# Global rows by TENSOR_REDUCE, global values scaled on ScalarE, w_in behind v's fifth transfer, and a newly planned order, in local and global attention with a softplus MLP

## The chip, the cores and the metric

The kernel runs on one core of one Trainium2 chip. The metric is device time in microseconds, the median of several runs. Beside it stands one profiled execution with its trace; all numbers of the trace below come from that one.

The engines, as the profile names them: PE (TensorE: matmuls; PEld are its weight loads), DVE (VectorE), ACT (ScalarE), POOL (GpSimd) and SP (SyncE, here only a queue for DMA). Each runs its own instructions in order and waits on semaphores for the others.

## The reference

Attention over 8 batches of 8 heads, 576 positions, head size 64. Each position sees a window of 32 on both sides and 8 global positions; the global positions see everything and are seen by everything. An MLP with a softplus follows.

```python
def _attn_ref(q, k, v, global_idx) -> np.ndarray:
    window = 32
    scores = scale * np.matmul(q, k.transpose(0, 1, 3, 2))
    mask = np.abs(pos[:, None] - pos[None, :]) <= window
    mask = mask | is_global[:, None] | is_global[None, :]
    scores = np.where(mask, scores, -1000000000.0)
    scores = scores - np.max(scores, axis=-1, keepdims=True)
    attn = np.exp(scores)
    attn = attn / (np.sum(attn, axis=-1, keepdims=True) + 1e-09)
    return np.matmul(attn, v).astype(np.float32)

def _moe_ref(x, w_in, w_out) -> np.ndarray:
    h = x @ w_in
    g = np.maximum(h, 0.0) + np.log1p(np.exp(-np.abs(h)))
    return (g @ w_out).astype(np.float32)
```

`x` is the attention's output as 4608 tokens of 512 channels; `w_in` is 512 by 2048, `w_out` 2048 by 512.

## The kernel before

**Tiling.** A block is 32 positions of one batch with all 8 heads; four blocks make a pair `n` (128 rows, 36 pairs), four pairs make a tile `m` of 512 tokens (9 tiles). For a pair PE computes scores `s` (L960), DVE adds the mask into `st` (L964) and takes the row maximum `m` (L977; for the first four pairs from `s`, L975), POOL subtracts it (L983), ACT takes the exponential (L996, L992), DVE the sum `sm` and its reciprocal `rs` (L1003, L1005), POOL multiplies into `pn` (L1011), DVE transposes into `pt` (L1020). PE then forms the values `xo` (L1122) of a piece of a tile, `xT` is copied out (L622, the line of a helper), and the MLP follows: `h` (L1157, weights `win`), softplus `g` on ACT (L1163), `o` (L1168, weights `wout`), a copy `osb` and a store.

**The global path**, once per batch `b`, gives the attention of the 8 global positions. PE computes their scores `sg` (L860) in four pieces; DVE takes four maxima `gm` (L870) and joins them by two into `gnb` (L871); ACT takes exponentials into `pg` (L877); DVE transposes `pg` into `pgt` (L882) and copies the one-hot rows `own`, which tell where a global position lies, beside it (L884); PE multiplies with v, `ov` (L893), which also sums the weights and gathers v; the odd blocks' half is copied to `odd` (ACT or DVE), DVE adds the even half (L904), takes the reciprocal `grs` (L905) and scales into `vg` (L906). PE's `xo` needs `vg`, and v in bf16, `vb`, which POOL, DVE or ACT casts from the landed `stage2`.

ACT holds one table at a time: exponential or softplus; a switch is an ACT_TABLE_LOAD.

**Loads.** SP issues q, k and v of a batch; v in eight transfers, four of them for each half of the heads (L370). The weights go through POOL's queue: `w_in` in four pieces behind a small copy `seen` (L1236) that waits until v's second transfer of batch 0 has landed, `w_out` in four pieces behind a like copy for the last q of batch 1. Batch 1's loads on SP stand behind a tiny read of `w_in`'s second piece (`trail`, L653), v of batch 1 behind one of `w_out`'s second.

**The order.** Nothing is emitted as it is written. Every piece of work is a job with costs in ns (begin to next, begin to end) for each engine that may do it, with dependencies, a rank and the buffers and PSUM banks that it opens. `_Order.run` takes the job that can start first by its own clock, the rank breaking ties, and so fixes the engine of each job and the order of each engine. `DRAWS` disturbs ranks and gives some jobs a `hold`, their earliest start after what they wait for. `stall` models that PE reads its own instructions in blocks of 256, which are asked for at instruction 130 and needed at 442, then every 256 further, and take the times in `SLOW`. Idle stretches of PE up to 34 us are filled with matmuls on nothing (`warm`, L630).

Of the kernel before, what the change touches and what calls it, by code (L numbers as in the profile page):

```python
# [282 lines left out]
def kernel(  # L283
# [49 lines left out]
    DRAWS = (14983,88331,14823,89303,53658,33409,90561,3122,88327,96354,15096,44709,93792,39917,99844,80902,91136,6210,80107,65898,80098,28397,56976,32762,97173,31915,3965,53549,42749,35567,44889,97522,97233,49667,59144,12623,98256,77249,34126,)  # L333
# [347 lines left out]
    def add_cast(b, w):  # L681
# [6 lines left out]
        for h in range(2):  # L688
# [158 lines left out]
    def add_global(b, gate):  # L847
# [15 lines left out]
        def mx(e, hs):  # L863
# [7 lines left out]
            V.tensor_tensor(out=PS["gnb", b][:, hs[0]:hs[-1] + 1], in0=m[:, hs[0]:hs[-1] + 1, 0], in1=m[:, hs[0]:hs[-1] + 1, 1], op=OP.min)  # L871
# [9 lines left out]
        def tpg(e, m0, m1):  # L881
            V.transpose(out=pgt[:, m0:m1].rearrange("p m i h -> p (m i h)").bitcast(I32),  # L882
                        in_=pg[:, m0:m1].rearrange("p m i h -> p (m i h)").bitcast(I32))
            V.tensor_copy(pgt[:, m0:m1, NG:2 * NG, :].rearrange("p m g h -> p m (g h)"),  # L884
                          own[:, m0:m1].rearrange("p m g h -> p m (g h)"))
# [15 lines left out]
        def gv(e):  # L901
            rs = sb.tile([P, 1], FP32, tag="grs", name="grs")
            both = PS["odd", b]
            V.tensor_tensor(out=both[:], in0=PS["ov", b, 0][:, :], in1=both[:], op=OP.add)  # L904
# [1 line left out]
            V.tensor_scalar(out=vg[i][:], in0=both[:, 0:2 * D], scalar1=rs[:, 0:1], scalar2=None, op0=OP.mult)  # L906
# [434 lines left out]
```

## Time and profile before

| what | us |
|---|---|
| median of three runs | 355.19 |
| the three runs | 352.88, 355.19, 356.19 |
| the profiled execution | 355.85 |
| its span, from first to last instruction | 354.1 |
| mean granted TensorE clock | 0.971 of full speed |

In the page, busy time is a share of the span, and a group's line gives the count, the busy time, the mean of one in ns, the idle time of the engine just before, and what ended that idle time. In a timeline a row gives start, duration, engine, line, operation, output and input, the count, and in brackets the idle time before with its releaser. In the waits, a row gives who waited for whom, the total, the number of times and the longest.

### The profile page before, as it was taken

Reading aid. Unit: us, or ns where it says so; the run is one execution under the profiler, and the core shown is the slowest. Engines: PE = TensorE matmul, PEld = TensorE weight load, DVE = VectorE, ACT = ScalarE, POOL = GpSimd, SP = SyncE. Lnnn points to the kernel's source line nnn. Section 1 sums busy time; section 2 is a strip of 40 time slices with the busy share of each in tenths; the row PEclk is TensorE's granted clock in tenths of the full one; section 3 lists DMA queues with packets and bytes.
Section 4 is the critical chain, followed back from the end, with each engine's and each line's share of the span. In section 5 each row is a group of like instructions: output and inputs, shape, how many; then the busy total and the mean of one; then the engine's idle time right before and its main releaser. Section 6 shows DMA issues by size and latency. Waiting matters only on the chain.

```text
span 354.1 us, 12267 instructions
## 1 busy us (share of the span) xinstructions
PE 323.5 (91%) x5327; PEld 171.8 (49%) x5327; DVE 238.9 (67%) x397; ACT 235.8 (67%) x463; POOL 188.5 (53%) x167
## 2 busy tenths in 40 slices
PE   6828769989997999899979998999999989999996
PEld 3414748458744444444435444544454454445453
DVE  7767668893899799994898089967991691061000
ACT  5658746969793779358926693679576837754631
POOL 6555627656296685569459535875954342060000
PEclk9667989999999999999999999999999999999999
DMA  7999799994999988925977098610100010010011
GB/s 194 198 204 255 142 213 165 173 187 108 180 181 199 193 157 140 189 66 120 183 131 181 15 178 153 164 35 31 61 33 31 22 70 32 0 59 33 30 44 74
DMA packets 168733, 42.74 MB, mean 121 GB/s; under 512 B 153192, under 2 KB 165736, under 8 KB 168680
## 3 DMA queue, kind: packets, MB, share of 16 engines
q1 hardware_dynamic: 160664, 28.33, 45.3%
q0 software_dynamic: 6144, 10.49, 12.3%
q10 hardware_dynamic: 1872, 3.15, 2.4%
q8 instruction: 41, 0.67, 0.8%
q14 instruction: 12, 0.10, 0.1%
HBM read 36.71 MB, written 9.44 MB: 130 GB/s over the span
## 4 chain that ended last, share of the span: by engine, by line
PE 51%; DVE 25%; SPq 10%; ACT 6%; DMA 4%; issue 3%; DVEq 0%; ACTq 0%
PE h L1157 30%; PE o L1168 13%; DVE sm L1003 7%; SPq L365 5%; DVE pt L1020 4%; PE xo L1122 4%; DMA stage<-in_v_dram 4%; SPq L370 3%; DVE pgt L884 3%; DVE vg L906 3%; PE s L960 2%; ACT st L996 2%; DVE gm L870 1%; DVE pgt L882 1%; ACT g L1163 1%
## 5 line engine op out<-in xcount | busy, mean ns | idle before, releaser
L1168 PE MATMUL o<-wout,g 128*128 128x512 bf16 (+1 forms) x592 | 134.0, 374 | 0.0
L1157 PE MATMUL h<-xT,win 128*128 128x512 bf16 (+2 forms) x768 | 133.8, 328 | 0.0
L1011 POOL TENSOR_TENSOR pn<-st,rs 128x1024 bf16<-128x1024 f32 (+1 forms) x39 | 68.1, 1754 | 81.5 <-DVE rs L1005 69.4
L1163 ACT ACTIVATE g<-h 128x512 bf16<-128x512 f32 (+2 forms) x192 | 86.0, 499 | 33.5 <-PE h L1157 30.3
L1157 PEld LDWEIGHTS <-win 128*128 128x128 bf16 x768 | 69.1, 98 | 56.4 <-issue 1.1
L1168 PEld LDWEIGHTS <-g 128*128 128x128 bf16 x592 | 55.2, 98 | 61.2 <-issue 1.4
L983 POOL TENSOR_TENSOR st<-st,m 128x1024 f32<-128x1024 f32 x32 | 60.3, 1894 | 29.4 <-DVE m L977 29.4
L1003 DVE TENSOR_REDUCE sm<-st 128x8 f32<-128x1024 f32 x32 | 38.0, 1188 | 18.3 <-ACT st L996 18.1
L964 DVE TENSOR_TENSOR st<-s,mask 128x512 f32<-128x512 f32 x64 | 40.7, 675 | 5.1 <-PE s L960 5.0
L622 ACT COPY osb<-o 128x512 f32<-128x512 f32 (+1 forms) x37 | 21.1, 572 | 28.3 <-PE o L1168 22.8
L977 DVE TENSOR_REDUCE m<-st 128x8 f32<-128x1024 f32 x32 | 38.3, 1207 | 0.2
L996 ACT ACTIVATE st<-st 128x1024 f32<-128x1024 f32 x32 | 32.5, 1057 | 1.4 <-POOL pn L1011 0.9
L622 ACT CAST xT<-xo 128x512 bf16<-128x512 f32 (+2 forms) x25 | 11.8, 528 | 22.2 <-PE xo L1122 22.1
L1020 DVE STREAM_TRANSPOSE pt<-pn 128x512 int32<-128x512 int32 x36 | 24.6, 688 | 1.7 <-POOL pn L1011 1.6
L870 DVE TENSOR_REDUCE gm<-sg 128x1 f32<-128x320 f32 (+1 forms) x32 | 12.4, 448 | 12.8 <-PE sg L860 12.7
L1180 POOL DMA_DIRECT2D out_dram<-osb x24 | 14.1, 589 | 11.0 <-ACT osb L622 5.9
L717 DVE STREAM_TRANSPOSE qx<-qb 128x1152 int32<-128x1152 int32 x6 | 8.2, 1370 | 16.8 <-ACT qb L615 13.6
L960 PE MATMUL s<-kx,qx 64*32 64x128 bf16 x1152 | 15.5, 227 | 2.7 <-issue 2.7
L960 PEld LDWEIGHTS <-qx 64*32 64x32 bf16 x1152 | 10.4, 93 | 13.7 <-issue 12.8
L893 PE MATMUL ov<-vb,pgt 32*32 32x129 bf16 x576 | 7.0, 230 | 11.0 <-DVE pgt L884 11.0
L1163 ACT ACT_TABLE_LOAD x10 | 12.8, 1283 | 3.9 <-PE h L1157 3.8
L1122 PE MATMUL xo<-pt,vb 32*64 32x96 bf16 (+2 forms) x1328 | 14.5, 211 | 0.9 <-issue 0.9
(122 smaller groups left out, 316.0 us busy)
## 6 DMA issues: line engine op xcount, KB each, us to landing
stage<-in_v_dram SPq DMA_DIRECT2D x64, 144.0 KB, 4.3
stage<-in_k_dram SPq DMA_DIRECT2D x48, 144.0 KB, 3.7
stage<-in_q_dram SPq DMA_DIRECT2D x48, 144.0 KB, 3.7
out_dram<-osb POOLq DMA_DIRECT2D x24, 256.0 KB, 3.3
out_dram<-osb ACTq DMA_DIRECT2D x11, 256.0 KB, 2.0
stage<-in_q_dram SPq DMA_DIRECT2D x4, 512.0 KB, 5.2
stage<-in_k_dram SPq DMA_DIRECT2D x4, 512.0 KB, 7.0
win<-in_moe_w_in_dram POOLq DMA_DIRECT2D x4, 512.0 KB, 8.2
```

What stands on the lines that cost most here:

```text
L622: {"ACT": nc.scalar.copy, "DVE": V.tensor_copy, "POOL": nc.gpsimd.tensor_copy}[e](out, in_)
L960: nc.tensor.matmul(out=PS["s", n, g][quad(a ^ g), x, :], lhsT=qx[b % 2][rows(g), a, j * BL:(j + 1) * BL], rhs=kx[b % 2][rows(g), a, e0 * B ...
L964: V.tensor_tensor(out=PS["st", n][:, h, :, :], in0=PS["s", n, h][:, :, :], in1=mask[:, h, j0:j0 + PB, :, :].rearrange("p j s i -> p j (s i ...
L977: V.reduce_max(out=m[:], in_=flat(PS["st", n], h0, h1), axis=AX)
L983: nc.gpsimd.tensor_tensor(out=t, in0=t, in1=over(PS["m", n, y][:], SL * BL), op=OP.subtract)
L996: nc.scalar.activation(out=t, in_=t, func=AF.Exp)
L1003: V.reduce_sum(out=sm[:], in_=flat(PS["st", n], h0, h1), axis=AX)
L1011: on(e).tensor_tensor(out=PS["pn", n][:, :, :, h0:h1].rearrange("p x s h -> p h x s"), in0=PS["st", n][:, h0:h1], in1=PS["rs", n, y][:].re ...
L1020: V.transpose(out=bass.AP(base.tensor, base.offset, ap=[list(base.ap[0]), [2 * STEP, PB // 2], [STEP + BL // 2, 2], [1, SL * BL]]), in_=PS ...
L1157: nc.tensor.matmul(out=h[:, :], lhsT=w_in_t[c // 4][:, kd, c % 4 * P:(c % 4 + 1) * P], rhs=PS["xT", m][:, kd, lo:hi], start=(kd == 0), sto ...
L1163: nc.scalar.activation(out=PS["g", m, c][:, lo:hi], in_=PS[key][:, lo_of(c, hi - lo)], func=AF.Softplus)
L1168: nc.tensor.matmul(out=PS["o", m, ns, a][:, :], lhsT=PS["g", m, kf][:, ns * P:(ns + 1) * P], rhs=w_out_t[kf // 4][:, kf % 4, a:z], start=( ...
```

## The change

- The copy of the one-hot rows beside `pgt` becomes a maximum over groups of one element (TENSOR_REDUCE), with the same result.
- The two maxima of a head are joined by a TENSOR_REDUCE over pairs, no longer by an element-wise minimum of two strided operands.
- `gv` is split. DVE adds and takes the reciprocal (`both`); the scaling into `vg` is a multiplication on ACT.
- The copy that lets `w_in` start waits for v's fifth transfer, and the planner gives it a hold of 1100 ns.
- The planner's times for PE's instruction blocks go by six stages, and its costs for casts of v in batch 0, `odd`, `pn` on DVE and small `h` are other ones. With a new `DRAWS` it makes another order.

```diff
-    SLOW = (170000, 4600, 3600)
+    SLOW = ((29000, 6500), (37000, 4200), (46000, 5000), (62000, 4000), (150000, 4800), (1e9, 3800))
...
-                until, early, later = self.SLOW
-                last = max(here + (early if here < until else later), last + self.FETCH)
+                last = max(here + next(took for until, took in self.SLOW if here < until), last + self.FETCH)
...
-    DRAWS = (14983,88331,14823, ...
+    DRAWS = (72935,40158,93434, ...
...
-                cost = {"POOL": (1150, 1250), "DVE": (660, 740)}
+                cost = {"POOL": (1150, 1250), "DVE": (760, 850)}
...
-            V.tensor_tensor(out=PS["gnb", b][:, hs[0]:hs[-1] + 1], in0=m[:, hs[0]:hs[-1] + 1, 0], in1=m[:, hs[0]:hs[-1] + 1, 1], op=OP.min)
+            V.tensor_reduce(out=PS["gnb", b][:, hs[0]:hs[-1] + 1], in_=m[:, hs[0]:hs[-1] + 1, :], axis=AX, op=OP.min)
...
-            V.tensor_copy(pgt[:, m0:m1, NG:2 * NG, :].rearrange("p m g h -> p m (g h)"),
-                          own[:, m0:m1].rearrange("p m g h -> p m (g h)"))
+            V.reduce_max(out=pgt[:, m0:m1, NG:2 * NG, :].rearrange("p m g h -> p m (g h)"),
+                         in_=own[:, m0:m1].rearrange("p m g h -> p m (g h)").unsqueeze(3), axis=AX)
...
         def gv(e):
-            rs = sb.tile([P, 1], FP32, tag="grs", name="grs")
-            both = PS["odd", b]
-            V.tensor_tensor(out=both[:], in0=PS["ov", b, 0][:, :], in1=both[:], op=OP.add)
-            V.reciprocal(rs[:], both[:, 2 * D:2 * D + 1])
-            V.tensor_scalar(out=vg[i][:], in0=both[:, 0:2 * D], scalar1=rs[:, 0:1], scalar2=None, op0=OP.mult)
+            nc.scalar.mul(vg[i][:], PS["odd", b][:, 0:2 * D], PS["grs", b][:, 0:1])
+
+        def both(e):
+            t = PS["odd", b]
+            V.tensor_tensor(out=t[:], in0=PS["ov", b, 0][:, :], in1=t[:], op=OP.add)
+            rs = PS["grs", b] = sb.tile([P, 1], FP32, tag="grs", name="grs")
+            V.reciprocal(rs[:], t[:, 2 * D:2 * D + 1])
...
-        T["odd", b] = o.add({"ACT": (320, 420), "DVE": (400, 480)}, odd, [T["ov", b]] + (had(("gv", b - 2)) if b >= 2 else []), rank=rank - 1, uses=[("ov", b, 1)])
+        T["odd", b] = o.add({"ACT": (440, 540), "DVE": (510, 600)}, odd, [T["ov", b]] + (had(("gv", b - 2)) if b >= 2 else []), rank=rank - 1, uses=[("ov", b, 1)])
-        T["gv", b] = o.add({"DVE": (640, 730)}, gv, [T["odd", b]] + [T["val", x] for x in old_vals(b - 2)],
-                           rank=rank - 1, uses=[("ov", b, 0)])
+        T["both", b] = o.add({"DVE": (380, 460)}, both, [T["odd", b]], rank=rank - 1, uses=[("ov", b, 0)])
+        T["gv", b] = o.add({"ACT": (290, 390)}, gv, [T["both", b]] + [T["val", x] for x in old_vals(b - 2)], rank=rank - 1)
...
-            job = o.add({"POOL": (1040, 1040), "DVE": (640, 720)} if n < TP else pool(1905 * g // 8 + 90 * (g < 8)), lambda e, y=y: no(e, y), [job], rank=at,
+            job = o.add({"POOL": (1040, 1040), "DVE": (1000, 1080)} if n < TP else pool(1905 * g // 8 + 90 * (g < 8)), lambda e, y=y: no(e, y), [job], rank=at,
...
-                    T["first", m, c] = o.add(mm(KD, max(hi - lo, 150)), lambda e, c=c, k=key, a=lo, z=hi: first(e, c, k, a, z),
+                    T["first", m, c] = o.add(mm(KD, hi - lo), lambda e, c=c, k=key, a=lo, z=hi: first(e, c, k, a, z),
...
-    T["held"] = o.add(pool(190), lambda e: nc.gpsimd.tensor_copy(seen[quad(1), 0, :], stage[2][quad(1), 0, 0, 0:1]), [T["half", 0, 0]], rank=0)
+    T["held"] = o.add(pool(190), lambda e: nc.gpsimd.tensor_copy(seen[quad(0), 0, :], stage[2][quad(0), 1, 0, 0:1]), [T["half", 0, 0]], rank=0, hold=1100)
```

The order has moved at these places, among many. After the change most line numbers are one lower or one higher. POOL at the start, from the copy that waits for v; `win` are the pieces of `w_in`, `vb` is v in bf16. Before:

```order
L1236 COPY seen<-stage_62 32x1
L1219 DMA win_132<-in_moe_w_in_dram 128x4x512
L1219 DMA win_133<-in_moe_w_in_dram 128x4x512
L1011 TENSOR_TENSOR pn<-st,rs 128x512
L1219 DMA win_134<-in_moe_w_in_dram 128x4x512
L1011 TENSOR_TENSOR pn<-st,rs 128x512 x2
L1219 DMA win_135<-in_moe_w_in_dram 128x4x512
```

Now:

```order
L1237 COPY seen<-stage_62 32x1
L1220 DMA win_132<-in_moe_w_in_dram 128x4x512
L1012 TENSOR_TENSOR pn<-st,rs 128x512
L1220 DMA win_133<-in_moe_w_in_dram 128x4x512
L621 CAST vb_66<-stage_62 128x18x64
L1220 DMA win_134<-in_moe_w_in_dram 128x4x512
L1220 DMA win_135<-in_moe_w_in_dram 128x4x512
```

The second piece has moved behind the first `pn`, and a half of v is cast here, between the second piece and the third.

DVE at the same time, from the join of the global maxima to the one-hot rows of batch 0. Before:

```order
L871 TENSOR_TENSOR gnb<-gm 128x2
L1005 RECIPROCAL rs<-sm 128x4
L622 CAST vb_66<-stage_62 128x18x64
L1005 RECIPROCAL rs<-sm 128x4
L622 CAST vb_66<-stage_62 128x18x64
L1020 STREAM_TRANSPOSE pt<-pn 128x2x2x128
L882 STREAM_TRANSPOSE pgt<-pg 128x320
L884 COPY pgt<-own 128x10x16
L882 STREAM_TRANSPOSE pgt<-pg 128x256
L884 COPY pgt<-own 128x8x16
```

Now:

```order
L870 TENSOR_REDUCE gnb<-gm 128x2
L1006 RECIPROCAL rs<-sm 128x4
L621 CAST vb_66<-stage_62 128x18x64
L1012 TENSOR_TENSOR pn<-st,rs 128x512
L881 STREAM_TRANSPOSE pgt<-pg 128x320
L883 TENSOR_REDUCE pgt<-own 128x10x16
L881 STREAM_TRANSPOSE pgt<-pg 128x256
L883 TENSOR_REDUCE pgt<-own 128x8x16
```

DVE casts only one half of v, takes a `pn`, and leaves the first `pt` for later. On PE the 72 matmuls of `ov` of this batch stand together now (40 and 32 before, with a pair's scores between), followed by that pair's scores and six fillers, where five stood.

DVE in the global path of batch 4, between the transpose of `pg` and the adds that free banks for `xo`. Before:

```order
L882 STREAM_TRANSPOSE pgt<-pg 128x576
L884 COPY pgt<-own 128x18x16
L1020 STREAM_TRANSPOSE pt<-pn 128x2x2x128
L1003 TENSOR_REDUCE sm<-st 128x8
L1005 RECIPROCAL rs<-sm 128x8
L904 TENSOR_TENSOR odd<-ov,odd 128x129
L905 RECIPROCAL grs<-odd 128x1
L906 TENSOR_SCALAR vg_74<-odd,grs 128x128
L1020 STREAM_TRANSPOSE pt<-pn 128x2x2x128
```

Now:

```order
L881 STREAM_TRANSPOSE pgt<-pg 128x576
L883 TENSOR_REDUCE pgt<-own 128x18x16
L1021 STREAM_TRANSPOSE pt<-pn 128x2x2x128
L1004 TENSOR_REDUCE sm<-st 128x8
L1006 RECIPROCAL rs<-sm 128x8
L1021 STREAM_TRANSPOSE pt<-pn 128x2x2x128
L905 TENSOR_TENSOR odd<-ov,odd 128x129
L907 RECIPROCAL grs<-odd 128x1
```

The scaling is gone from DVE. On ACT it stands behind what the engine does in between, in this pass the last two exponentials of the pairs, the copy of `odd`, an `osb` copy and two small casts:

```order
L876 ACTIVATE pg<-sg,gnb 128x256 x2
L621 COPY osb<-o 128x512
L997 ACTIVATE st<-st 128x1024 x2
L621 COPY odd<-ov 64x129 x2
L621 COPY osb<-o 128x512
L621 CAST kx_71<-pick 128x40x8
L621 CAST qg_73<-pick 128x4x8
L901 ACTIVATE vg_74<-odd,grs 128x128
```

On PE, between `sg` and `ov` of batch 2, 34 matmuls of `o` stood, and now 24.

More of the change, by code (lines that the diff above doesn't have):

```diff
@@ L332 @@
     WARM = 34000
-    DRAWS = (14983,88331,14823,89303,53658,33409,90561,3122,88327,96354,15096,44709,93792,39917,99844,80902,91136,6210,80107,65898,80098,28397,56976,32762,97173,31915,3965,53549,42749,35567,44889,97522,97233,49667,59144,12623,98256,77249,34126,)
+    DRAWS = (72935,40158,93434,22620,33917,21303,34118,320,94210,20417,67588,27929,89332,44699,91926,34025,24655,51950,14931,28279,84849,57431,36627,86191,5081,90161,11244,23579,42329,10910,63620,38114,46230,63800,92924,3977,28773,26540,3374,59821,)
     AHEAD = [0, 0] + [1] * (NT - 2) + [0]
```

## The prediction

> **What bounds the kernel now.** I read the page's busy shares first, then who TensorE (PE) waited for, then the two stretches in which it waited, engine by engine.
>
> ```profile
> span 354.1 us, 12267 instructions
> PE 323.5 (91%) x5327; PEld 171.8 (49%) x5327; DVE 238.9 (67%) x397; ACT 235.8 (67%) x463; POOL 188.5 (53%) x167
> ```
>
> PE works for 323.5 of 354.1 us, so at most its 30.6 idle us, and what it runs slowly, can be won. DVE, at 67%, matters only where PE waits for it. The waits of PE, summed (us, times, longest):
>
> ```profile
> PE ov L893 <- DVE pgt L884: 11.0, 7, 6.3
> PE xo L1122 <- DVE st L964: 3.1, 4, 1.3
> PE s L960 <- issue: 2.7, 1, 2.7
> PE xo L1122 <- DVE pt L1020: 2.3, 4, 0.9
> PE pick L754 <- DVE qx L622: 0.9, 1, 0.9
> PE xo L1122 <- issue: 0.9, 1, 0.9
> PE xo L1122 <- DVE rs L1005: 0.6, 1, 0.6
> PE xo L1122 <- DVE vg L906: 0.6, 1, 0.6
> ```
>
> The largest `ov` wait (6.3) is at the start. The other six, 11.0 - 6.3 = 4.7 us, and the `xo` waits for `st`, `pt` and `vg`, 3.1 + 2.3 + 0.6 = 6.0 us, belong to the seven later passes of the global path: 10.7 us, one and a half per pass. "issue" is PE waiting for its own instructions. Now the operations that the change replaces (ns minimum/median/maximum), and one pass, batch 4, on DVE and POOL:
>
> ```profile
> L884 DVE COPY pgt<-own x9: 197/1434/2102, 25.4 to 282.3; 128x288 bf16<-128x288 bf16 x7, 128x160 bf16<-128x160 bf16 x1, 128x128 bf16<-128x128 bf16 x1
> L906 DVE TENSOR_SCALAR vg<-odd,grs x8: 287/1452/2199, 30.4 to 288.0; 128x128 bf16<-128x128 f32 x8
> L871 DVE TENSOR_TENSOR gnb<-gm x8: 160/161/961, 19.2 to 278.5; 128x2 f32<-128x2 f32 x8
> L1003 DVE TENSOR_REDUCE sm<-st x32: 1167/1172/1221, 64.7 to 313.9; 128x8 f32<-128x1024 f32 x32
> ...
> 174.57 3.75 POOL L1011 TENSOR_TENSOR pn<-st,rs 128x1024 bf16<-128x1024 f32 x2 [4.95 <-DVE rs L1005]
> 176.81 1.59 DVE L884 COPY pgt<-own 128x288 bf16<-128x288 bf16 x1
> 178.46 0.80 PE L893 MATMUL ov<-vb,pgt 32*32 32x129 bf16 x72 [0.65 <-DVE pgt L884]
> 180.54 1.89 POOL L1011 TENSOR_TENSOR pn<-st,rs 128x1024 bf16<-128x1024 f32 x1 [1.70 <-DVE odd L904]
> 180.76 1.75 DVE L906 TENSOR_SCALAR vg<-odd,grs 128x128 bf16<-128x128 f32 x1
> ```
>
> A copy of 0.20 us takes up to 2.10, a scaling of 0.29 up to 2.20, and in both rows the DVE instruction ends with POOL's: 176.81 + 1.59 = 178.40 against 174.57 + 3.75 = 178.32, and 180.76 + 1.75 = 182.51 against 180.54 + 1.89 = 182.43. These operations wait out the POOL instruction that they meet. The 32 sums by TENSOR_REDUCE (L1003) vary by 0.05 us, wherever POOL stands. So the excess is a wait, and it lies on the chain `pgt`, `ov`, `vg`, `xo`.
>
> **One-hot copy and maxima by TENSOR_REDUCE.** No row reduces groups of one element. The nearest:
>
> ```profile
> L512 DVE TENSOR_REDUCE dup<-same 128x8 f32<-128x64 f32 x1 | 0.2, 220 | 0.0
> L975 DVE TENSOR_REDUCE m<-s 128x4 f32<-128x512 f32 x8 | 5.3, 680 | 1.0 <-PE s L960 1.0
> ...
> 12.69 0.63 ACT L615 ACTIVATE qb<-stage 128x512 bf16<-128x512 f32 x1 [1.06 <-DMA stage<-in_q_dram]
> 42.68 0.41 ACT L615 ACTIVATE qb<-stage 128x256 bf16<-128x256 f32 x1
> ```
>
> From 64 to 512 elements 0.46 us are added, 1.03 ns each: 288 elements make 0.45 us, 160 and 128 make 0.32 and 0.29. Ends: 0.22 (as for 64) and 1.17 (L1003); I take 0.45, since the line passes on both sides of it. Per pass the copy's median 1.43 becomes 0.45, a gain of 1.0. The first pass's two copies (0.20 each) lose 0.2 together. The tiny minimum (L871) saves 0.8 in one pass, nothing in the others.
>
> The Trainium skill, "VectorE: DVE Perf Modes", section "The perf-mode tier table", speaks against it: a reduction has only the single-rate mode, a bf16 copy in SBUF four times that. By that page alone, as an estimate, the reduction would lose about 0.2 us a pass, and term 1 would shrink to what `vg` gives; the measured copies of 1.43 decide otherwise. "SBUF — State Buffer", section "Who interferes with whom", says that a reduction never contends with GpSimd on this chip, and a copy may; L884 and L1003 agree.
>
> **Scaling by ACT.** A scaling in SBUF takes ACT 0.63 us for 512 elements and 0.41 for 256, 0.86 ns each, so 128 make 0.30; the ends are 0.19 (0.41 less the 0.22 between the two rows) and 0.41. DVE loses 1.45 per pass, ACT gains 0.30, plus a hop. ACT is in order: `vg` now stands behind exponentials or `osb` copies. `xo` is behind it.
>
> Together a pass's DVE chain shortens by 1.0 + 1.45 = 2.4 us against a mean PE wait of 10.7 / 7 = 1.5. With the old order all would go. The new one gives some back: in batch 2's pass 24 `o` matmuls instead of 34 stand between `sg` and `ov`, ten times 0.216 (rate below) = 2.2 us less cover, against 1.0 for `pgt` and 0.8 for `gnb` that DVE sheds ahead of `ov` there: 0.4 is uncovered. I let 0.4 stay in each of the seven passes, 2.8 in all. **Term 1: -7.9** (ends 0 and -10.7).
>
> **w_in later, v's second half to POOL.** The start, from the chain, ACT, DVE, POOL and PE:
>
> ```profile
> 14.16 9.37 DMA stage<-in_v_dram
> 14.89 1.76 POOL L1219 DMA_DIRECT2D win<-in_moe_w_in_dram  x2 [0.39 <-issue]
> 17.86 1.04 POOL L1011 TENSOR_TENSOR pn<-st,rs 128x512 bf16<-128x512 f32 x1 [1.22 <-DVE rs L1005]
> 19.49 1.94 ACT L877 ACTIVATE pg<-sg,gnb 128x320 bf16<-128x320 f32 x4
> 19.36 0.85 DVE L622 CAST vb<-stage 128x1152 bf16<-128x1152 f32 x1
> 23.55 0.76 DVE L622 CAST vb<-stage 128x1152 bf16<-128x1152 f32 x1 [3.26 <-DMA stage<-in_v_dram]
> 24.23 0.70 DVE L1020 STREAM_TRANSPOSE pt<-pn 128x512 int32<-128x512 int32 x1
> 24.86 0.47 DVE L882 STREAM_TRANSPOSE pgt<-pg 128x320 int32<-128x320 int32 x1
> 25.48 0.44 DVE L882 STREAM_TRANSPOSE pgt<-pg 128x256 int32<-128x256 int32 x1
> 25.62 0.74 PE L893 MATMUL ov<-vb,pgt 32*32 32x129 bf16 x40 [6.28 <-DVE pgt L884]
> 28.38 2.31 PE L630 MATMUL warm<-pgt 128*128 128x512 bf16 x5
> 30.76 0.33 PE L1122 MATMUL xo<-pt,vg 32*64 32x128 bf16 x8
> 32.28 1.31 DVE L1011 TENSOR_TENSOR pn<-st,rs 128x512 bf16<-128x512 f32 x1
> ```
>
> v's last transfer takes 9.4 us because two pieces of `w_in` follow it within a microsecond. DVE stands still for it for 3.26 us, with everything behind it. Afterwards `w_in` starts behind the fifth transfer, its second piece behind a `pn`, and DVE casts only v's first half. DVE from 19.36: cast 0.85, `pn` 1.31, which ends at 21.5, just after ACT's `pg` (21.43); then 0.47 + 0.32 + 0.44 + 0.29, so both `pgt` pieces are there at 23.0 instead of 25.48 + 0.44 + 0.20 = 26.1. PE did `ov` and `s` from 25.62 to 28.38, 2.8 us; then it has six fillers instead of five (0.46 each, 2.8). With a hop, 23.2 + 2.8 + 2.8 = 28.8: `xo` starts there instead of at 30.76, if `vg` and `pt` are ready, which the order has ahead of the fillers' end. **Term 2: -1.9** (ends 0 and -3.1, the whole shift of `pgt`). If v came no earlier than now, POOL's cast would hold `ov`, and the term is gone. POOL issues the second `w_in` piece behind the `pn` that ends at 18.9, not by 14.89 + 1.76 = 16.65, and batch 1's loads follow that piece. I cost it at nothing, covered by v and the first piece, which keep the DMA busy; without that cover it costs up to 2.3 us.
>
> **Order planned with later fetches.** The planner's rule is that instructions 256 apart are asked for at 130 and needed at 442. PE's three waits for instructions lie within four matmuls of such points. The PE work between asking and need, counted in the order with these rates
>
> ```profile
> 307.99 11.65 PE o L1168 x54
> ...
> 47.81 0.31 PE L960 MATMUL s<-kx,qx 64*32 64x128 bf16 x16 [2.66 <-issue]
> 48.93 2.72 PE L1157 MATMUL h<-xT,win 128*128 128x256 bf16 x12
> 51.99 1.49 PE L1157 MATMUL h<-xT,win 128*128 128x256 bf16 x12
> ```
>
> (0.216 us for 512 columns, in proportion for fewer, 0.80 / 72 = 0.011 for small ones, some 0.03 for transposes) was 4.75, 3.48 and 4.70 us at the three points; now it is 5.04, 5.36 and 5.08. The waits of 0.9, 0.9 and 2.7 fall by 0.3, 0.9 and 0.4. Against that one point at batch 1's `xo` comes down to 3.9; the next covers that met no wait there were 4.6, so up to 0.7 may come, and I add 0.3. Of the wait of `xo` for `rs` (0.6), 0.5 goes: more `h` stands near it. After the long stall twelve matmuls took 2.72 for 1.49; I count none of that. **Term 3: -1.6 - 0.5 + 0.3 = -1.8** (ends +3.9, one new stall of 2.7 with its cold 1.2, and -6.3, all four waits and the 1.2).
>
> **Sum:** -7.9 - 1.9 - 1.8 = -11.6 from the profiled run's 355.85 us (span 354.1 and 1.75 around it): 344.25, given as 344.3. The median shown, 355.19, is 0.7 lower, within the runs' scatter of 3.3, so I make no correction.
>
> **Rivals.**
> - *Half goes.* The waits pass to what is next: `st` adds that free the PSUM banks for `xo`, POOL's `pn` (1.89 each), or ACT, where `vg` queues. For it: 3.1 us of the `xo` waits already name `st`. Against: those adds stand behind `vg` on DVE and move with it. Half of each term: 355.85 - 5.8 = 350.
> - *All goes.* The better ends: -10.7 - 3.1 - 6.3 gives 335.8.
> - *The replacement does not work.* A reduction writing 288 single results costs 1.2 to 1.4 us (the end above, or the copy's own median), and ACT's `vg` comes as late as DVE's did. Then terms 2 and 3 alone, less what the denser passes lose (some 2): 354. Nothing in the rows shows a cost per group; nothing excludes it.
> - *Slower.* Denser passes run into instruction loads: less `o` between `sg`, `ov` and `xo` brings asking and need together. One such stall costs 2.7 + 1.2 = 3.9 us; with all three terms otherwise kept, three of them bring the time back to 356 and four to 360, so it decides from four on, more than one in every second pass. Against it: past 60 us the trace shows none, and only one point falls below the covers that met none.
>
> **How the numbers follow.** Chances: forecast 0.55, by itself 341 to 348; all goes 0.07; half 0.22; doesn't work 0.09; slower 0.07. The range 340 to 352 leaves out most of "all goes", the upper part of "doesn't work" and "slower", about 2 in 10. About 1% (3.6 us) is what a measurement of this kernel can tell from no change. Faster by more: 0.55 + 0.07 + 0.19 of the half case = 0.81; within it: 0.03 + 0.09 = 0.12; slower 0.07.
>
> **What would show it.** Term 1: reductions into `pgt` of 0.4 to 0.5 us with little spread, `vg` on ACT near 0.3, and the waits of `ov` and `xo` past 60 us summing to about 3. Term 2: no wait of DVE or POOL for v near 23 us, first `xo` near 29. Term 3: the 2.7 us wait before `s` shorter and no new one later. Wrong if the reductions take over 1 us, if "issue" rows of PE appear past 60 us, or if `xo` waits for ACT's `vg`.

## The result, and the profile after

| kernel | median us | runs | profiled execution | its span | clock |
|---|---|---|---|---|---|
| before | 354.12 | 352.88 to 356.19 (4) | 355.85 | 354.1 | 0.971 |
| after | 344.42 | 343.85 to 345.51 (4) | 343.85 | 342.1 | 0.979 |

The ratio is 0.9724, with a 95% interval of 0.9664 to 0.9784: about 9.7 us faster. `before` has one run more here (353.04) than was shown ahead of the prediction. The ratios below rest on the single runs, not on the medians, so that the two can differ by up to 0.3 per cent. The prediction was 344.3. That its steps were as good as its sum does not follow; most of what comes below is about that.

From the page of the profile after, the span, the busy times and the granted clock in 40 slices:

```profile
span 342.1 us, 12180 instructions
PE 317.8 (93%) x5277; PEld 173.9 (51%) x5328; DVE 220.8 (65%) x390; ACT 235.8 (69%) x467; POOL 189.6 (55%) x168
PEclk9698998999999999999999999999999999999999
```

DVE is busy for 18 us less than before. PE has 5328 weight loads but only 5277 matmuls: 51 matmul records are missing, 36 of them `o` (556 rows instead of 592). This matters for reading the waits of PE after 60 us (us in total, times, longest):

```profile
PE o L1169 <- issue: 3.4, 21, 0.2
PE ov L892 <- DVE pgt L883: 1.8, 1, 1.8
PE s L961 <- issue: 0.9, 1, 0.9
PE pick L776 <- ACT qb L614: 0.7, 1, 0.7
PE o L1169 <- ACT g L1164: 0.5, 1, 0.5
PE sg L859 <- ACT g L1164: 0.3, 1, 0.3
PE pick L789 <- DVE picked L621: 0.3, 1, 0.3
```

The first row is 21 gaps of 0.16 us. I take them for the holes of missing records and not for waits, since only the traces that lack records have such a row. Of the 10.7 us for which `ov` and `xo` waited here before, 1.8 are left, all in the pass of batch 2, at 101.8. Small waits elsewhere have come in: 0.7 + 0.5 + 0.3 + 0.3 = 1.8 us of `pick`, `o` and `sg`, and 0.9 of `s` that the profile puts down to "issue", which this text reads as PE waiting for its own instructions. The replaced operations after (ns minimum, median, maximum):

```profile
L883 DVE TENSOR_REDUCE pgt<-own x9: 285/452/453, 21.2 to 272.9; 128x288 bf16<-128x288 bf16 x7, 128x160 bf16<-128x160 bf16 x1, 128x128 bf16<-128x128 bf16 x1
...
L901 ACT ACTIVATE vg<-odd,grs x8: 401/402/408, 24.8 to 277.1; 128x128 bf16<-128x128 f32 x8
...
L870 DVE TENSOR_REDUCE gnb<-gm x8: 156/157/157, 19.0 to 267.7; 128x2 f32<-128x4 f32 x8
```

The reductions have no spread left. And the start, after, on POOL and PE in order of time:

```profile
17.17 0.18 POOL L1237 COPY seen<-stage 32x1 f32<-32x1 f32 x1 [4.32 <-DMA stage<-in_v_dram]
19.30 1.20 POOL L1220 DMA_DIRECT2D win<-in_moe_w_in_dram  x1
20.50 1.30 POOL L621 CAST vb<-stage 128x1152 bf16<-128x1152 f32 x1
21.84 0.86 PE L892 MATMUL ov<-vb,pgt 32*32 32x129 bf16 x72 [2.87 <-POOL vb L621]
23.53 1.47 PE L629 MATMUL warm<-pgt 128*128 128x512 bf16 x6
25.88 0.26 PE L1123 MATMUL xo<-pt,vg 32*64 32x128 bf16 x8 [0.88 <-DVE pt L1021]
```

`ov` starts at 21.84 instead of 25.62, the first `xo` at 25.88 instead of 30.76. This is 4.9 us where the prediction had 1.9. By these two traces alone, the start gave some 4 to 5 us and the later passes 7. The experiments show that the first of these numbers is mostly not the change's: v was late in this execution of before, and between the first `ov` and the first `xo` the granted clock was 0.50 here and 1.00 in after.

### The profile page after: what moved, and what is told of

The parts are those of the page before. It is cut to its first block, busy times and chain, and to the rows that moved or that the text cites. A ratio compares the mean times of both kernels' runs of the same rounds, so it can differ in the third digit from the quotient of the medians.

```text
span 342.1 us, 12180 instructions
## 1 busy us (share of the span) xinstructions
PE 317.8 (93%) x5277; PEld 173.9 (51%) x5328; DVE 220.8 (65%) x390; ACT 235.8 (69%) x467; POOL 189.6 (55%) x168
## 4 chain that ended last, share of the span: by engine, by line
PE 70%; SPq 12%; issue 5%; DMA 5%; ACT 4%; POOL 2%; DVE 0%; POOLq 0%; ACTq 0%
PE o L1169 32%; PE h L1158 29%; SPq L364 8%; PE xo L1123 4%; SPq L369 3%; PE s L961 2%; DMA win<-in_moe_w_in_dram 2%; DMA stage<-in_q_dram 2%; ACT g L1164 1%; PE ov L892 1%; SPq L418 1%; DMA stage<-in_v_dram 1%; PE pick L776 1%; SPq L414 1%; POOL win L1220 1%
## 5 line engine op out<-in xcount | busy, mean ns | idle before, releaser
L1169 PE MATMUL o<-wout,g 128*128 128x512 bf16 (+1 forms) x556 | 127.2, 374 | 4.5 <-issue 3.4
L1158 PEld LDWEIGHTS <-win 128*128 128x128 bf16 x768 | 70.7, 101 | 57.4 <-DMA win<-in_moe_w_in_dram 1.8
L984 POOL TENSOR_TENSOR st<-st,m 128x1024 f32<-128x1024 f32 x32 | 60.4, 1896 | 27.1 <-DVE m L978 26.6
L1021 DVE STREAM_TRANSPOSE pt<-pn 128x512 int32<-128x512 int32 x36 | 24.9, 694 | 6.9 <-POOL pn L1012 6.8
L720 DVE STREAM_TRANSPOSE kx<-kb 128x1152 int32<-128x1152 int32 x6 | 8.2, 1362 | 13.1 <-ACT kb L621 13.1
L876 ACT ACTIVATE pg<-sg,gnb 128x320 bf16<-128x320 f32 (+1 forms) x32 | 15.0, 589 | 0.5 <-ACT osb L621 0.5
L621 DVE CAST xT<-xo 128x512 bf16<-128x512 f32 (+2 forms) x22 | 10.6, 522 | 7.1 <-PE xo L1123 7.0
L716 DVE STREAM_TRANSPOSE qx<-qb 128x1152 int32<-128x1152 int32 x6 | 8.2, 1364 | 10.7 <-ACT qb L614 10.1
```

The costliest lines, as they stand in the source:

```text
L621: {"ACT": nc.scalar.copy, "DVE": V.tensor_copy, "POOL": nc.gpsimd.tensor_copy}[e](out, in_)
L984: nc.gpsimd.tensor_tensor(out=t, in0=t, in1=over(PS["m", n, y][:], SL * BL), op=OP.subtract)
L1158: nc.tensor.matmul(out=h[:, :], lhsT=w_in_t[c // 4][:, kd, c % 4 * P:(c % 4 + 1) * P], rhs=PS["xT", m][:, kd, lo:hi], start=(kd == 0), sto ...
L1169: nc.tensor.matmul(out=PS["o", m, ns, a][:, :], lhsT=PS["g", m, kf][:, ns * P:(ns + 1) * P], rhs=w_out_t[kf // 4][:, kf % 4, a:z], start=( ...
```

## The experiments

Twelve experiments ran, one of them (e9) the kernel before once more. "Old order" is the kernel before with its order untouched, "new order" the kernel after. The columns give the ratio to the kernel before run beside it, the start of the first `ov` and of the first `xo`, the waits of PE for its own instructions from 20 to 60 us (rows "issue" of 0.5 us and more), and the waits of `ov` and `xo` for other engines past 60 us, all in us and from one trace each. The medians of `before` beside them reach from 351.77 to 354.89, so ratios of different groups compare only to within some 0.9 per cent. The traced execution of e2 took 347.75 us, 4.6 above the median of its runs, so its trace is left out.

| run | order | w_in behind v's | copy, join | vg | ratio (95%) | ov | xo | instr. | ov, xo |
|---|---|---|---|---|---|---|---|---|---|
| before | old | 2nd | old | DVE | 1 | 25.6 | 30.8 | 3.6 | 10.7 |
| e9 | old | 2nd | old | DVE | 1.0013 (0.9975 to 1.0052) | 22.8 | 27.9 | 3.3 | 10.8 |
| e10 | old | 5th | old | DVE | 1.0072 (1.0036 to 1.0107) | 24.4 | 29.5 | 5.0 | 10.8 |
| e5 | old | 2nd | reductions | DVE | 0.9794 (0.9728 to 0.9860) | 22.7 | 27.8 | 5.6 | 3.4 |
| e6 | old | 2nd | old | ACT | 0.9797 (0.9711 to 0.9882) | 22.8 | 27.4 | 4.6 | 5.0 |
| e3 | old | 2nd | reductions | ACT | 0.9718 (0.9627 to 0.9808) | 24.9 | 30.1 | 4.4 | 0 |
| e4 | old | 5th | reductions | ACT | 0.9735 (0.9631 to 0.9840) | 24.8 | 30.0 | 3.0 | 0 |
| e1 | new | 5th | old | DVE | 0.9949 (0.9904 to 0.9993) | 22.6 | 28.0 | 4.6 | 7.2 |
| e2 | new | 2nd | reductions | ACT | 0.9703 (0.9611 to 0.9796) | | | | |
| e7 | new | 5th | copy old | ACT | 0.9706 (0.9625 to 0.9787) | 22.6 | 27.5 | 3.8 | 4.8 |
| e8 | new | 5th | reductions | DVE | 0.9703 (0.9634 to 0.9771) | 22.3 | 27.6 | 4.4 | 1.8 |
| e11 | new | 5th | old | ACT | 0.9853 (0.9803 to 0.9904) | 22.8 | 27.7 | 2.2 | 6.1 |
| after | new | 5th | reductions | ACT | 0.9724 (0.9664 to 0.9784) | 21.8 | 25.9 | 2.3 | 1.8 |
| e12 | both | 5th | reductions | ACT | 0.9775 (0.9723 to 0.9826) | 22.4 | 27.1 | 3.1 | 1.6 |

### Order or operations (e1 to e4)

e1 is the changed kernel with the three operations as before, e2 the changed kernel with the copy that releases `w_in` as before. e3 is the kernel before with the three new operations and its order kept; e4 is e3 with `w_in` behind v's fifth transfer.

e1, against the kernel after:

```diff
-            V.tensor_reduce(out=PS["gnb", b][:, hs[0]:hs[-1] + 1], in_=m[:, hs[0]:hs[-1] + 1, :], axis=AX, op=OP.min)
+            V.tensor_tensor(out=PS["gnb", b][:, hs[0]:hs[-1] + 1], in0=m[:, hs[0]:hs[-1] + 1, 0], in1=m[:, hs[0]:hs[-1] + 1, 1], op=OP.min)
...
-            V.reduce_max(out=pgt[:, m0:m1, NG:2 * NG, :].rearrange("p m g h -> p m (g h)"),
-                         in_=own[:, m0:m1].rearrange("p m g h -> p m (g h)").unsqueeze(3), axis=AX)
+            V.tensor_copy(pgt[:, m0:m1, NG:2 * NG, :].rearrange("p m g h -> p m (g h)"),
+                          own[:, m0:m1].rearrange("p m g h -> p m (g h)"))
...
-            nc.scalar.mul(vg[i][:], PS["odd", b][:, 0:2 * D], PS["grs", b][:, 0:1])
+            V.tensor_scalar(out=vg[i][:], in0=PS["odd", b][:, 0:2 * D], scalar1=PS["grs", b][:, 0:1], scalar2=None, op0=OP.mult)
```

e2, against the kernel after:

```diff
-nc.gpsimd.tensor_copy(seen[quad(0), 0, :], stage[2][quad(0), 1, 0, 0:1])
+nc.gpsimd.tensor_copy(seen[quad(1), 0, :], stage[2][quad(1), 0, 0, 0:1])
```

e3, against the kernel before (join and copy as the change has them, and):

```diff
-            V.tensor_scalar(out=vg[i][:], in0=both[:, 0:2 * D], scalar1=rs[:, 0:1], scalar2=None, op0=OP.mult)
+            nc.scalar.mul(vg[i][:], both[:, 0:2 * D], rs[:, 0:1])
```

e4, against e3:

```diff
-nc.gpsimd.tensor_copy(seen[quad(1), 0, :], stage[2][quad(1), 0, 0, 0:1])
+nc.gpsimd.tensor_copy(seen[quad(0), 0, :], stage[2][quad(0), 1, 0, 0:1])
```

> The changed kernel in its own order, with the one-hot rows copied, the maxima joined by an element-wise minimum and the values scaled on DVE, as before (the scaling stands in DVE's row where the plan has it on ACT). Contention theory: each pass's DVE chain grows by about 2.4 us, as the copy and the scaling wait out POOL's instruction again, and since the new order has less work between sg, ov and xo, PE waits for most of it: 7 to 9 us lost, 351 to 354 us, with copies and scalings of 1 to 2 us. Order theory (the gain comes from the new order alone): at most 346 us.

> The changed kernel with w_in released by v's second transfer again; nothing else moves in the order. Gate theory: v lands 3 to 4 us later (near 23), POOL's cast and with it ov and the first xo come 2 to 3 us later, while the 1.5 us wait of h for w_in goes: 346 to 347.5 us. Rival (the start is set by PE's instruction loads and batch 1's transfers further on): 343.5 to 345 us, no difference.

> The kernel before in its old order, with the reductions and the scaling on ACT. Contention theory: the 10.7 us of waits of ov and xo past the start nearly all go, since every pass sheds more DVE time (1.7 to 3.4 us) than PE waited there (1.0 to 2.4): 345 to 348 us. Order theory: 353 to 355 us.

> As the one before, and w_in behind v's fifth transfer. Gate theory: DVE's 3.3 us stand at v's second half shrinks to 1 or less, the first xo comes 2 to 3 us earlier: 1.5 to 3 us less than the one before, 343 to 346 us, as good as the changed kernel without its order. Rival: no difference to the one before.

The medians were 349.97, 343.13, 342.99 and 344.84, beside 351.77 for the kernel before. The operations on the old order (e3) bring all of the gain. The new order with its gate and the old operations (e1) brings half a per cent. Where the gate stands shows in neither pair: e2 against after, e4 against e3. So the gate theory missed twice (346 to 347.5 for e2; 1.5 to 3 us below e3 for e4), e1 lies between its two theories (351 to 354, at most 346), and e3 came out 2 us below the contention theory's 345. The waits of PE past 60 us in e3 are down to these two rows; `ov` and `xo` wait for nothing any more:

```profile
PE h L1157 <- issue: 0.4, 1, 0.4
PE h L1157 <- ACT xT L622: 0.2, 1, 0.2
```

But order and operations do not add up. On the old order the operations take the ratio from 1 to 0.972, on the new one from 0.995 to 0.972. The trace of e1 shows what the new order does with the old operations in batch 2's pass (DVE, POOL, ACT and PE):

```profile
101.72 1.90 POOL L984 TENSOR_TENSOR st<-st,m 128x1024 f32<-128x1024 f32 x1
102.19 1.44 DVE L870 TENSOR_TENSOR gnb<-gm 128x2 f32<-128x2 f32 x1
...
103.67 1.86 ACT L876 ACTIVATE pg<-sg,gnb 128x320 bf16<-128x320 f32 x4 [0.41 <-DVE gnb L870]
...
107.60 2.02 DVE L883 COPY pgt<-own 128x288 bf16<-128x288 bf16 x1
107.61 1.91 POOL L1012 TENSOR_TENSOR pn<-st,rs 128x1024 bf16<-128x1024 f32 x1
...
109.67 0.85 PE L892 MATMUL ov<-vb,pgt 32*32 32x129 bf16 x72 [4.69 <-DVE pgt L883]
```

The minimum over 128x2 values ends at 102.19 + 1.44 = 103.63, with the POOL instruction that ends at 101.72 + 1.90 = 103.62; the copy ends at 109.62, with POOL's at 109.52. Two such waits stand in one chain, and 24 `o` matmuls cover less of it than 34 did. The same place after:

```profile
97.18 0.16 DVE L870 TENSOR_REDUCE gnb<-gm 128x2 f32<-128x4 f32 x1
...
101.30 0.45 DVE L883 TENSOR_REDUCE pgt<-own 128x288 bf16<-128x288 bf16 x1
...
101.81 0.80 PE L892 MATMUL ov<-vb,pgt 32*32 32x129 bf16 x72 [1.84 <-DVE pgt L883]
```

1.28 and 1.57 us shorter, and the wait shorter by 4.69 - 1.84 = 2.85, their sum.

A long wait costs more than itself here. Behind the one of 4.69 us the granted clock was 0.54 (110.0 to 113.3 us), and fourteen `o` matmuls took 4.78 us; behind the 1.84 of after it was 1.00, and thirteen took 2.97. The other long wait of e1, 2.21 us of `xo` for `vg` at 75.15, was followed by a clock of 0.54 to 0.61 until 80. In before, whose waits past 60 us are 1.5 at most each, the clock was 1.00 from 64 to 330 us. So two stretches of some 3.4 us at half clock, up to 1.7 us each as an estimate, can take back most of what e1's 7.2 us of waits are below the 10.7 of before.

### Which operation (e5 to e8)

e5 is e3 without its edit of `vg`; e6 is the kernel before with that edit alone; e7 and e8 are the kernel after with one operation as before.

```diff
-            nc.scalar.mul(vg[i][:], both[:, 0:2 * D], rs[:, 0:1])
+            V.tensor_scalar(out=vg[i][:], in0=both[:, 0:2 * D], scalar1=rs[:, 0:1], scalar2=None, op0=OP.mult)
```

That was e5, against e3; e6, against the kernel before:

```diff
-            V.tensor_scalar(out=vg[i][:], in0=both[:, 0:2 * D], scalar1=rs[:, 0:1], scalar2=None, op0=OP.mult)
+            nc.scalar.mul(vg[i][:], both[:, 0:2 * D], rs[:, 0:1])
```

e7, against the kernel after:

```diff
-            V.reduce_max(out=pgt[:, m0:m1, NG:2 * NG, :].rearrange("p m g h -> p m (g h)"),
-                         in_=own[:, m0:m1].rearrange("p m g h -> p m (g h)").unsqueeze(3), axis=AX)
+            V.tensor_copy(pgt[:, m0:m1, NG:2 * NG, :].rearrange("p m g h -> p m (g h)"),
+                          own[:, m0:m1].rearrange("p m g h -> p m (g h)"))
```

e8, against the kernel after:

```diff
-            nc.scalar.mul(vg[i][:], PS["odd", b][:, 0:2 * D], PS["grs", b][:, 0:1])
+            V.tensor_scalar(out=vg[i][:], in0=PS["odd", b][:, 0:2 * D], scalar1=PS["grs", b][:, 0:1], scalar2=None, op0=OP.mult)
```

> The old order with both reductions (one-hot rows, join of the maxima); vg stays on DVE. The old order with all three new operations came to 342.99 against 351.77, 8.8 faster. Theory A, each operation's meeting with POOL is a cost by itself and the waits of PE past 60 us belong to the operation ahead of them: the 4.7 us of ov waits go, the 6.0 of xo waits stay, 347. Theory B, one chain per pass with slack, where the scaling is the last link: the reductions alone only bring vg earlier to the next POOL instruction, which it waits out, 350 or more. Theory C, only DVE's load counts (busy 238.9 to 220.1, of which the copy gives 6.9 and the join 0.8): 348. The trace tells A from C by where PE still waits past 60 us: under A before xo alone.

> The old order with vg scaled on ACT; the copy of the one-hot rows and the join stay as before. Theory A: the 6.0 us of xo waits go, the ov waits of 4.7 stay, 346. Theory B (scaling is the last link, the copy before it has slack): nearly all goes, 343 to 344. Theory C (load alone, 10.4 of DVE's 18.8 us): 347.

> The changed kernel with the one-hot rows copied again on DVE; join and vg stay new. All three old operations on this order cost 350.0 - 344.4 = 5.6 us. Theory A (sums): the stall of 4.7 us that the pass with 24 o matmuls showed with the old operations comes back and little else, 348. Theory B: ov waits by the copy's excess in that pass alone, 1 to 2 us, 345 to 346. The trace shows the wait of ov near 102 us: 1.8 in the changed kernel, 4.7 with the old operations.

> The changed kernel with vg scaled on DVE again; both reductions stay. Theory A (sums): what the copy did not cost, 5.6 less the 3.6 of e7, about 346.5; theory B: xo waits for vg where it meets a long POOL instruction, in this order mostly hidden behind o matmuls: 345 to 346, with one xo wait of 2 us at most, as with the old operations (2.2).

The medians were 347.00, 346.42, 344.01 and 343.08; before had 354.89 in this group. On the old order theory A comes nearest (347 and 346): each operation takes away waits that stand behind it. Past 60 us PE's waits in e5 are

```profile
PE xo L1122 <- DVE st L964: 1.9, 3, 0.9
PE xo L1122 <- DVE pt L1020: 1.5, 3, 0.8
```

and in e6

```profile
PE ov L893 <- DVE pgt L884: 4.7, 6, 1.5
...
PE xo L1122 <- DVE pt L1020: 0.3, 1, 0.3
```

With the reductions the 4.7 of `ov` go and of the 6.0 of `xo` 3.4 stay; with `vg` on ACT the 4.7 stay to the tenth and the `xo` waits go. Each alone is worth 2.1 and 2.0 per cent, both together 2.8, with intervals of some 0.8 on either side; whether a part is shared can't be read from that. On the new order both theories expected a loss, and neither e7 nor e8 has one that can be measured, though the trace of e7 has the wait of `ov` at 3.4 instead of 1.8. This is the copy's excess in that pass alone (2.02 - 0.45 = 1.57), as theory B said.

### The start, the gate and the join (e9 to e11)

e9 is the kernel before, unchanged, profiled again. e10 is the kernel before with the gate alone, the edit of e4:

```diff
-nc.gpsimd.tensor_copy(seen[quad(1), 0, :], stage[2][quad(1), 0, 0, 0:1])
+nc.gpsimd.tensor_copy(seen[quad(0), 0, :], stage[2][quad(0), 1, 0, 0:1])
```

e11 is e7 with the old join besides:

```diff
-            V.tensor_reduce(out=PS["gnb", b][:, hs[0]:hs[-1] + 1], in_=m[:, hs[0]:hs[-1] + 1, :], axis=AX, op=OP.min)
+            V.tensor_tensor(out=PS["gnb", b][:, hs[0]:hs[-1] + 1], in0=m[:, hs[0]:hs[-1] + 1, 0], in1=m[:, hs[0]:hs[-1] + 1, 1], op=OP.min)
```

> The kernel before, profiled a second time, to see whether its start is the same. Theory V: v's last transfer of batch 0 comes late only in some executions, so the 3.26 us that DVE waited for it, on which term 2 stands, are no fixed cost. Two runs with the old loads (e5, e6) showed no such wait and ov at 22.7 instead of 25.6. Then the profile shows either no wait for v, ov near 22.7 and a time near 351, or a wait of some 3 us, ov near 25.6 and a time near 355; the times of the kernel before have reached from 349.5 to 356.2 so far. Theory T (term 2 as predicted): the wait of about 3 us is there whenever w_in follows v's second transfer.

> The old order and the old operations, w_in behind v's fifth transfer: the gate alone. Theory T: v's wait goes, but POOL's two issues of w_in now stand ahead of pn and pt, which took ov to 24.8 in e4: 0 to 1 us faster than before, 353 to 354 where before has 354. Theory V: the gate only takes the late executions away and puts POOL's issues in their place, so its times scatter less (within 3 us) and lie at the upper group of before's, 353 to 355.

> The changed kernel with the copy of the one-hot rows and the element-wise minimum back on DVE; vg stays on ACT. All three old operations cost 5.6 us on this order, the copy alone and vg alone showed nothing (344.0, 343.1). Theory J: the thin pass of batch 2 makes the difference, where the minimum waited out POOL for 1.44 us (0.16 as a reduction) and the copy for 2.02 (0.45): the wait of ov comes back to 4.7, PE runs slowly after it (fourteen o matmuls took 4.78 us there, 3.0 at full speed), and the time is 347 to 348; the rest, to 350.0, is the wait of xo for vg (2.2). Theory K: vg on DVE is what cost, and the copy and the minimum stay hidden: 344 to 345.

The medians were 352.45, 354.68 and 346.83, before in this group 353.18. The start of e9, the same program as before, on POOL, DVE and PE:

```profile
14.71 1.76 POOL L1219 DMA_DIRECT2D win<-in_moe_w_in_dram  x2 [0.39 <-issue]
17.62 1.04 POOL L1011 TENSOR_TENSOR pn<-st,rs 128x512 bf16<-128x512 f32 x1 [1.15 <-DVE rs L1005]
20.40 1.08 DVE L622 CAST vb<-stage 128x1152 bf16<-128x1152 f32 x1 [0.35 <-DMA stage<-in_v_dram]
22.78 0.74 PE L893 MATMUL ov<-vb,pgt 32*32 32x129 bf16 x40 [3.50 <-DVE pgt L884]
27.93 0.27 PE L1122 MATMUL xo<-pt,vg 32*64 32x128 bf16 x8
```

DVE waits 0.35 us for v, not 3.26, `ov` starts 2.8 us earlier and the span is 3.5 us shorter (350.6; the execution took 352.33, where theory V said near 351). This is theory V: v's late landing in the first profile belongs to that execution. e3 had it too (2.49), e5 and e6, with the same loads, did not. The start of e10:

```profile
17.61 0.18 POOL L1236 COPY seen<-stage 32x1 f32<-32x1 f32 x1 [4.62 <-DMA stage<-in_v_dram]
17.73 1.76 POOL L1219 DMA_DIRECT2D win<-in_moe_w_in_dram  x2
19.49 1.47 POOL L1011 TENSOR_TENSOR pn<-st,rs 128x512 bf16<-128x512 f32 x1
24.39 0.74 PE L893 MATMUL ov<-vb,pgt 32*32 32x129 bf16 x40 [5.42 <-DVE pgt L884]
29.53 0.33 PE L1122 MATMUL xo<-pt,vg 32*64 32x128 bf16 x8
```

v is not late in this trace, but POOL, which runs in order, stands in the gate for 4.62 us and issues two pieces of `w_in` before it comes to `pn`, at 19.49 instead of 17.62. `ov` and `xo` follow 1.6 us later than in e9. The gate alone costs 0.7 per cent, about 2.5 us, and its times still scatter by 4.6 (353.2 to 357.8), not within the 3 that theory V gave.

e11 comes nearest to theory J (347 to 348; K had 344 to 345). From e7 to e11 only the join of two values differs. In e7:

```profile
104.53 1.11 PE L892 MATMUL ov<-vb,pgt 32*32 32x129 bf16 x72 [3.40 <-DVE pgt L883]
```

And in e11:

```profile
97.04 1.92 POOL L984 TENSOR_TENSOR st<-st,m 128x1024 f32<-128x1024 f32 x1
97.51 1.46 DVE L870 TENSOR_TENSOR gnb<-gm 128x2 f32<-128x2 f32 x1
...
105.01 0.98 PE L892 MATMUL ov<-vb,pgt 32*32 32x129 bf16 x72 [4.71 <-DVE pgt L883]
```

The wait of `ov` in batch 2's pass goes from 3.4 to 4.7, by what the minimum waits for POOL. The intervals of the ratios do not overlap (0.9787 and 0.9803 are their near ends), but the size stays open: the ratios differ by 1.5 per cent, the medians by 2.8 us or 0.8 per cent, since before had 354.89 beside e7 and 353.18 beside e11, and e7's four runs reach from 341.39 to 346.38. Whether anything beyond the 1.3 us of the stall is due to the join, the two traces don't settle; the `o` matmuls behind the stall ran slowly in both (thirteen in 4.01 us, fourteen in 4.61, against thirteen in 2.97 after), at a granted clock of 0.50 from 106 to 108 us.

### Both orders' better half (e12)

The planner can be made to follow a given list of jobs and engines. e12 is the kernel after with such a list: the new order for all that the planner starts in its first 60 us, and behind it what is left, in the old order. `GIVEN` is a string of 1720 jobs.

```diff
+    o.given = [(int(x), dict(P='PE', A='ACT', V='DVE', G='POOL', D='DMA')[y]) for x, y in (z.split('.') for z in GIVEN.split())]
     for job in o.run(dict(PE=1200 if WARM else 3000, ACT=2600, DVE=2100, POOL=3400, DMA=2700)):
```

> The changed kernel's operations, gate and order for all that the planner starts within its first 60 us, and from there the old order. Theory S: the two orders are each better at one place, and so come out even: the new one reaches the first xo some 2 us earlier (27.5 to 28 with w_in behind v's fifth transfer, 29.5 to 30 on the old order with v late or that gate), the old one leaves 0.6 us of waits of ov and xo past 60 us where the new one leaves about 4, its pass of batch 2 having 34 o matmuls ahead of ov, not 24. Then both are had: 2 to 3.5 us below the 343.0 of the old order with the new operations and the 344.4 of the changed kernel, 340 to 341.5, with no wait of ov for pgt past 60 us. Theory N: the two are equal for other reasons, and joined orders leave new waits where they meet (60 to 70 us): 343 to 345.

The median was 345.65, beside 353.19, above what either theory gave (340 to 341.5, 343 to 345). What theory S foresaw happened at both places: the first `xo` at 27.1, and no wait of `ov` for `pgt` past 60 us. The time did not follow, since other waits came. PE past 60 us:

```profile
PE pick L776 <- ACT qb L614: 2.3, 1, 2.3
PE o L1169 <- ACT g L1164: 1.4, 1, 1.4
PE h L1158 <- ACT vb L621: 1.1, 1, 1.1
PE xo L1123 <- ACT vg L901: 1.0, 1, 1.0
```

The first and the third stand at 132.1 and 217.3 us, and e4, which has the old order and the same gate, has both at the same places (2.16 at 132.1, 1.13 at 217.8), while e3, without the gate, has no `pick` row and 0.4 us of "issue" at that `h`. In the 3.2 us after the `pick` wait the granted clock was 0.50 in e12 and e4, so this wait costs more than itself. What was late for it is a load. ACT in e12:

```profile
125.46 1.49 ACT L614 ACTIVATE qb<-stage 128x1152 bf16<-128x1152 f32 x1 [4.42 <-DMA stage<-in_q_dram]
```

In e3 this cast starts at 122.82 without a wait. The later gate moves the loads behind it: the tiny read that holds batch 1's loads comes at 27.19 in e12, 27.07 in e4 and 25.05 in e3, the one that holds batch 1's v at 51.62, 49.56 and 46.72. e4 and e3 differ by the gate alone. With the passes' own waits gone, PE now meets the loads. The `h` wait is another matter: the cast `vb` that it names began without a wait for a load in all three traces (215.82, 215.86 and 212.41), and its cause stays open. The list with the gate at v's second transfer was not tried.

## Why the prediction was right, and where it was not

**The sum.** That 344.25 came so near 344.42 is luck: two errors stood against each other. It started at 355.85, an execution with v late, 1.7 above the median of 354.12 (the medians of the kernel before in five groups were 351.8 to 354.9), and it took off 11.6, which is 1.9 more than the 9.7 measured. The operations alone make all of the 9.7 (e3: 2.8 per cent, 1.9 to 3.7), and terms 2 and 3, to which 3.7 us were given, show no gain on top of them (0.9718 without them, 0.9724 with them).

**Term 1, -7.9.** Right in mechanism: the DVE copy and the scaling wait out POOL, and the chain to `ov` and `xo` was the cost. Past 60 us the waits of `ov` and `xo` fell by 8.9, and 1.8 came in at `pick`, `o` and `sg`. The reduction takes 0.452 us where 0.45 was said; no cost per group. `vg` on ACT takes 0.402, not 0.30: the line through the two `qb` rows was 0.10 too low, and the upper end of the range, the 0.41 of 256 elements, was nearest. Those rows are scaled by a constant, `vg` by a value per partition; no run here shows the two side by side. The Trainium skill, "ScalarE: Activation LUTs", section "What ACT_TABLE_LOAD costs", gives 186 ns and 0.833 per element, and 93 for an operand that is one value per partition, which the reciprocal here is: as an estimate 0.386, and the eight passes (0.401 to 0.408) lie some 0.02 above it. "I let 0.4 stay in each of the seven passes" failed as a distribution: six passes have nothing, the thin one has 1.84. The count of 24 against 34 `o` had named this pass, but the sum for it (2.2 less 1.0 and 0.8) left out that `ov` waited there already, in the kernel before:

```profile
108.36 0.80 PE L893 MATMUL ov<-vb,pgt 32*32 32x129 bf16 x72 [1.47 <-DVE pgt L884]
```

With it the prediction's own terms give 0.4 + 1.5 = 1.9 (2.3 if the copy's 1.05 us in that pass replaces the median of 1.43). That 2.8 for seven passes lies near what PE waits now is luck. That the join "saves 0.8 in one pass, nothing in the others" was too little for the new order: there it saves 1.3 in that pass.

**Term 2, -1.9.** This is the step that failed, though `xo` came 4.9 us earlier between the two profiles. It took DVE's 3.26 us wait for v as a fixed cost; one more profile of the same kernel (e9) has 0.35, though two pieces of `w_in` follow v within a microsecond there too, so that they alone do not make v late. Against e9, whose `xo` starts at 27.93, five other traces with the new start have it at 27.1 to 28.0; only the one of after has 25.9. From the first `ov` to the first `xo` its granted clock was 1.00, and the stretch took 4.04 us with the six fillers in 1.47; in the twelve other traces of the table the clock was 0.50 to 0.69 and the stretch took 4.7 to 5.4, the fillers of e1 and e8 2.74. Why the clock was full in this execution stays open. The loads behind the later gate, costed "at nothing", came into play: after waits 0.7 us at `pick`, e4 and e12 2.2 and 2.3. Alone on the old order the gate costs some 2.5 us, of which 1.6 are POOL's `pn` behind it.

**Term 3, -1.8.** Not shown. It worked out the waits for instructions from PE's work between asking and need. With the same order and place they differ by execution. PE in e1, at `xo` and `s`:

```profile
33.97 0.33 PE L1123 MATMUL xo<-pt,vb 32*64 32x96 bf16 x26 [2.02 <-issue]
...
53.28 0.36 PE L961 MATMUL s<-kx,qx 64*32 64x128 bf16 x22 [2.59 <-issue]
```

And in e11, of the same order and gate:

```profile
33.34 0.32 PE L1123 MATMUL xo<-pt,vb 32*64 32x96 bf16 x26 [0.78 <-issue]
...
49.46 0.35 PE L961 MATMUL s<-kx,qx 64*32 64x128 bf16 x22 [0.61 <-issue]
```

After had 0.21 and 2.34 there. The sums (the column "instr.") are 3.0 to 5.6 on the old order, 4.2 in the mean of seven, and 2.2 to 4.6 with the new start, 3.4 in the mean of six. 0.8 us may lie in this, against the 1.3 of the prediction, but each trace differs from the next by more. The 0.5 of `xo` for `rs` went, on the old order with `vg` on ACT (e3, e6 have no such row) and on the new one without it too (e1, e8).

**The rivals.** "All goes" was true of the waits of `ov` and `xo` on the old order (e3) without bringing its 335.8, since that needed terms 2 and 3 as well. "Slower" needed four new stalls of 3.9 us; past 60 us the longest wait for instructions after is 0.9. "Half goes" named DVE's adds, POOL and ACT as what is late next; in e4 and e12 it was the loads, for 2.2 and 2.3 us. That the replacement does not work fell with the 0.452. Of the signs that were to speak against the prediction one came: an "issue" row past 60 us, 0.9 of `s`; `xo` waits for ACT's `vg` in e7, e11 and e12 (0.9 to 1.0), past 60 us not in after.

## What to carry to other kernels

Where an operation's time varies by ten between its minimum and its maximum, as the copy's did here, suspect a wait for another engine: look at what ends with it, and price its replacement by the chain behind it, pass by pass, since the pass with the least cover pays for all. A wait at the start of one trace is a cost only if a second trace of the same program has it, and this second trace is the cheapest experiment there is. When the waits in a loop are gone, what loads for the loop can decide, so moving a load to win at the start must be paid from there.

## What the runs showed of the hardware that was not expected

- A DVE minimum of two operands of 128x2 values took 1.44 us (0.16 in the other passes), ending within 0.02 us of the POOL instruction beside it. So an operation that reads next to nothing waited all the same. TENSOR_REDUCE for the same job took 0.156 to 0.157 in all eight passes. The Trainium skill, "SBUF — State Buffer", section "Who interferes with whom", says both: a DVE instruction with two inputs in SBUF contends with a GpSimd instruction that reads SBUF, a reduction never does. The traces agree, and the prediction had weighed only the copy by it.
- A TENSOR_REDUCE over groups of one element, 288 of them, took 0.452 us; writing each group's result cost nothing that shows.
- PE's wait "issue", read as a wait for its own instructions, ranged at one and the same instruction from 0.2 to 2.0 us (`xo`, five executions of the new start and the one of after), nothing in the program being different ahead of it but the operations of one pass; past 60 us it was 1.2 at most.
- Past 60 us, behind single waits of PE of 2.2 us and more (e1, e4, e7, e11, e12), the granted clock was about 0.5 for some 3.4 us. Behind shorter ones it stayed at 1.00 in before (1.5 at most) and after (1.84), but not in e8, where it fell to 0.50 behind one of 1.46.
- v's last transfer, behind the same transfers in the same queues, was waited for by 3.26 us in one execution and by 0.35 in another.
